# Preparing the input of two fused MLP layers in timed steps with buffers of its own, in a kernel of rotary attention and two wide layers

## The chip, the cores and the metric

One core of one Trainium2 chip. The metric is the device time of one execution in microseconds; for the kernel before it is the median of three runs. Where the text says TensorE, VectorE, ScalarE, GpSimd and SyncE, the profile's rows say PE (and PEld for its weight loads), DVE, ACT, POOL and SP.

## The reference

Attention with rotary embeddings over 4 batches, 8 heads, 576 positions and 64 dims, then two layers on the 2304 tokens of 512 dims, all in float32:

```python
q_rot, k_rot = (rotate(q), rotate(k))
scores = scale * np.matmul(q_rot, k_rot.transpose(0, 1, 3, 2))
attn = np.exp(scores - np.max(scores, axis=-1, keepdims=True))
attn = attn / (np.sum(attn, axis=-1, keepdims=True) + 1e-09)
x = (attn @ v)            # heads side by side: 2304 x 512
h = np.maximum(x @ w_in, 0.0);  x = h * h @ w_out              # layer 0, d_ff 2048
h = x @ w_in2;  x = (np.maximum(h, 0) + alpha * np.minimum(h, 0)) @ w_out2   # layer 1
```

## The kernel before

To keep float32's precision, each operand of a product is split into a high and a low part that TensorE takes at its fast rate, and a product is three matmuls: high by high, high by low, low by high. High parts are made by ACT (a copy that rounds), low parts by DVE (a subtraction).

*Attention* (`attention`) takes 16 pairs of heads, each in 9 steps of scores; a step's probabilities are transposed 4 steps later (L222, splits in L210 and L211) and the products with v (L267) follow. Unnormalised results go to `xd` in memory, the reciprocals of the sums to `rd`. From a number of steps after the last scores on (`FOLLOW`), each of its steps also lets the second part run one step further.

*The layers* (`moe`) are one list of units. A block is 384 of the 2304 tokens, so there are six; a unit is one block by one of 16 tiles of `w_in` (z = 0, L511 to L513) or `w_out` (z = 1, L529): 12 matmuls, 9 in layer 1's second half. Blocks 0 and 1 of layer 0 come first and take turns tile by tile (units 0 to 63); then each block has 32 units, blocks 2 to 5 of layer 0 (64 to 191), and all six of layer 1 (192 to 383). The loop over t issues at step t: the products of unit t, the split of g for unit t + 1 (`split_g`: gh on ACT L476, gl on DVE L477, two buffers each), the activation of unit t - 1 (`finish`: ACT relu L551, then the square on ACT L557 or POOL L559 by turns), and the jobs of the table for this t, later stages first. Steps with t < 2 run inside attention's last steps. PE, DVE, ACT and POOL keep program order from t = 2 on (`manual_schedule`; attention has it for PE alone); before that, and on SP throughout, the framework's scheduler sets the order.

*Weights* (`Weights`) arrive as float32 pairs of words that are converted in five stages at steps from a table: load two steps ahead (SP, L371), `convert` (DVE L380, L381, L382), `grow` one step later (ACT L387), `sign` two later (DVE L392, L393), `join` three later (ACT L399, L400, POOL L401). Layer 0's 32 weights come at 1.8 units each, from weight 26 on at 2 and not before unit 45, and stay in the chip's memory; layer 1's 32 are converted during blocks 2 to 5 at 2.9 units each into `wc` (two buffers), stored to memory (SP L447) and loaded back in block 5.

*The layers' input x* comes in four chunks of 128 dims a block. `prepare_x` does a chunk in one go: four loads (SP L493 xr, L495 r), add of two halves (DVE L496), product with r (POOL L497), xh (ACT L500), xl (DVE L501); for layer 1 a single load (L499) takes the place of loads, add and product. xr and r have one buffer each for blocks 0 and 1, later two for xr and one for r. Blocks 0 and 1 are prepared at t = -8 to -4; a later block's chunks at i = 4 to 7 of the z = 1 half of the block before it.

## Time and profile before

| | |
|---|---|
| median of three runs | 1254.2 us (1252.58 to 1254.74) |
| the profiled execution's own time | 1252.51 us |
| its span, first to last instruction | 1250.7 us |
| mean granted TensorE clock | 0.969 |
| busy: PE, DVE, ACT, POOL | 89%, 55%, 48%, 35% of the span |
| attention's part | to about 340 us |
| layer 0 | to about 849 us |
| layer 1 | to 1244.8 us |

A stage is read by the busy time of the engines in it and the granted clock; where TensorE is idle, the row of an instruction names in brackets how long its engine stood before it and whose end released it. An engine takes its instructions in order, so that one that waits holds all behind it.

### The profile page before, as it was taken

What the parts mean: (1) busy time and instruction counts of PE and PEld (TensorE: products, weight loads), DVE (VectorE), ACT (ScalarE), POOL (GpSimd) and SP (SyncE); (2) the same over time, 40 slices, a digit from 0 to 9 for tenths busy, and PEclk for the clock granted to TensorE, in tenths of its full rate; (3) what the DMA queues carried; (4) which work ended last, traced back from release to release, by engine and by line L of the source; (5) the groups of instructions that cost most, each with busy time, mean ns of one, the idle gap of its engine ahead of it and who ended that gap; (6) DMA issues with size and microseconds to landing.
All of it is one profiled execution on the core that took longest, in us unless ns stands there. A gap on an engine that the chain in (4) does not pass through costs nothing.

```text
span 1250.7 us, 18130 instructions
## 1 busy us (share of the span) xinstructions
PE 1118.2 (89%) x6480; PEld 1047.9 (84%) x6480; DVE 690.5 (55%) x1179; ACT 603.4 (48%) x1292; POOL 440.4 (35%) x404
## 2 busy tenths in 40 slices
PE   2899999999639878798897998999999999999998
PEld 2788988998529767798897997999898999989896
DVE  3788888888636787755756655032323232323332
ACT  2788878787516664555463553332323232322222
POOL 7965665621114442223242232103132222313040
PEclk9999999999869989999898998999999999999999
DMA  8776775654533344345655553883000101010101
GB/s 238 178 189 179 177 184 151 164 133 116 164 107 101 110 140 125 104 155 168 197 186 172 185 170 122 243 278 93 26 26 26 26 26 26 14 38 1 38 1 25
DMA packets 97497, 150.20 MB, mean 120 GB/s; under 512 B 21760, under 2 KB 66432, under 8 KB 97408
## 3 DMA queue, kind: packets, MB, share of 16 engines
q1 hardware_dynamic: 91792, 138.85, 39.1%
q10 hardware_dynamic: 5360, 10.07, 2.2%
q8 instruction: 51, 0.84, 0.3%
q14 instruction: 38, 0.31, 0.1%
q0 software_dynamic: 256, 0.13, 0.0%
HBM read 84.98 MB, written 35.73 MB: 97 GB/s over the span
## 4 chain that ended last, share of the span: by engine, by line
PE 61%; DVE 12%; POOL 8%; DMA 8%; issue 5%; ACT 5%; SPq 2%; ACTq 0%; POOLq 0%; DVEq 0%
PE py L529 24%; PE ph L511 9%; PE ph L512 9%; PE ph L513 9%; PE acc L267 3%; PE sc L201 3%; PE ps L222 2%; DVE m L381 2%; POOL xr L497 2%; DMA kraw<-in_k_dram 2%; DMA r<-r 2%; POOL w L401 2%; DMA xr<-x 2%; DVE w L382 1%; DVE ptl L211 1%
## 5 line engine op out<-in xcount | busy, mean ns | idle before, releaser
L511 PE MATMUL ph<-xh,w 128*128 128x384 f32 x768 | 260.4, 339 | 29.4 <-ACT xh L500 22.0
L512 PE MATMUL ph<-xl,w 128*128 128x384 f32 x768 | 259.5, 338 | 0.0
L513 PE MATMUL ph<-xh,w 128*128 128x384 f32 x768 | 258.7, 337 | 0.6 <-POOL w L401 0.6
L477 DVE TENSOR_TENSOR gl<-g,gh 128x384 fp32r<-128x384 f32 x192 | 109.7, 572 | 206.5 <-ACT gh L476 206.5
L555 POOL TENSOR_TENSOR g<-g,mn 128x384 f32<-128x384 f32 x96 | 100.3, 1045 | 297.1 <-DVE mn L554 297.1
L529 PE MATMUL py<-gh,w 128*128 128x384 f32 x640 | 178.6, 353 | 23.7 <-ACT gh L476 23.7
L551 ACT ACTIVATE g<-ph 128x384 f32<-128x384 f32 x192 | 93.5, 490 | 202.3 <-PE ph L513 194.7
L476 ACT ACTIVATE gh<-g 128x384 fp32r<-128x384 f32 x192 | 100.0, 521 | 184.0 <-PE py L529 151.8
L529 PE MATMUL py<-w,gh 128*128 128x512 f32 x576 | 177.4, 389 | 0.0
L511 PEld LDWEIGHTS ph<-xh,w 128*128 128x128 f32 x768 | 145.8, 190 | 33.8 <-ACT xh L500 24.0
L529 PEld LDWEIGHTS py<-gh,w 128*128 128x128 f32 x640 | 124.2, 200 | 28.3 <-ACT gh L476 28.3
L512 PEld LDWEIGHTS ph<-xl,w 128*128 128x128 f32 x768 | 145.7, 190 | 1.7 <-DVE xl L501 1.5
L513 PEld LDWEIGHTS ph<-xh,w 128*128 128x128 f32 x768 | 145.8, 190 | 0.9 <-POOL w L401 0.9
L401 POOL TENSOR_TENSOR w<-m,w 128x512 fp32r<-128x512 f32 x64 | 87.9, 1374 | 155.0 <-ACT w L399 136.0
L554 DVE TENSOR_SCALAR mn<-ph,al 128x384 f32<-128x384 f32 x96 | 59.3, 618 | 141.6 <-ACT g L551 135.9
L529 PEld LDWEIGHTS py<-w,gh 128*128 128x128 f32 x576 | 108.0, 188 | 22.2
L529 PE MATMUL py<-gl,w 128*128 128x384 f32 x320 | 115.5, 361 | 9.8 <-DVE gl L477 9.7
L205 ACT ACTIVATE p<-sc,nm 128x576 f32<-128x576 f32 x144 | 106.6, 741 | 25.7 <-DVE nm L204 18.9
L204 DVE TENSOR_REDUCE nm<-sc 128x1 f32<-128x576 f32 x144 | 105.8, 752 | 20.0 <-PE sc L201 18.6
L529 PE MATMUL py<-w,gl 128*128 128x512 f32 x288 | 112.2, 389 | 0.0
L211 DVE TENSOR_TENSOR ptl<-ps,pth 128x512 fp32r<-128x512 f32 (+1 forms) x160 | 99.7, 631 | 15.3 <-ACT pth L210 12.9
L210 ACT ACTIVATE pth<-ps 128x512 fp32r<-128x512 f32 (+1 forms) x160 | 86.9, 554 | 40.8 <-PE ps L222 40.1
(94 smaller groups left out, 1921.2 us busy)
## 6 DMA issues: line engine op xcount, KB each, us to landing
w<-in_moe_w_in_dram SPq DMA_DIRECT2D x32, 512.0 KB
w<-in_moe_w_out_dram SPq DMA_DIRECT2D x32, 512.0 KB
wk<-w SPq DMA_DIRECT2D x32, 512.0 KB
w<-wk SPq DMA_DIRECT2D x32, 512.0 KB
xr<-x SPq DMA_DIRECT2D x72, 192.0 KB
kH<-nat SPq DMA_DIRECT2D x64, 144.0 KB
qT<-nat SPq DMA_DIRECT2D x64, 144.0 KB
kL<-nat SPq DMA_DIRECT2D x64, 144.0 KB
```

The source lines that it names most:

```text
L204: V.tensor_reduce(out=nm, in_=sc[:, :, 0:SH], axis=AX.XY, op=ALU.max, negate=True)
L205: A.activation(out=Pt[n, i][:, j * S:(j + 1) * S].rearrange("p (a b) -> p a b", a=2), in_=sc[:, :, 0:SH], func=AF.Exp, bias=nm, accum_out= ...
L211: V.tensor_tensor(out=sl(lo), in0=src, in1=sl(hi).bitcast(F32), op=ALU.subtract)
L401: G.tensor_tensor(out=wc[:, 1], in0=m.bitcast(F32), in1=lo.bitcast(F32), op=ALU.mult)
L476: A.activation(out=hi, in_=g, func=AF.Copy)
L477: V.tensor_tensor(out=lo, in0=g, in1=hi.bitcast(F32), op=ALU.subtract)
L511: T.matmul(ph[:, :W], lhsT=wh[:, cs], rhs=xh, start=(c == 0), stop=False)
L512: T.matmul(ph[:, :W], lhsT=wh[:, cs], rhs=xl, start=False, stop=False)
L513: T.matmul(ph[:, :W], lhsT=wl[:, cs], rhs=xh, start=False, stop=(c == KC - 1))
L529: T.matmul(acc, lhsT=x, rhs=y, start=(s0 and k == 0), stop=(s1 and k == 2))
L551: A.activation(out=g, in_=ph, func=AF.Relu)
L555: G.tensor_tensor(out=g, in0=g, in1=mn, op=ALU.add)
```

## The change

FOLLOW is 1 instead of 5 and STEPS_AHEAD 8 instead of 7: the layers' steps begin with the second step after the last scores, at t = -9. Program order on PE, DVE, ACT and POOL begins there. `prepare_x` becomes four stages with steps of their own: `load_x`, `join_x` (the add now on POOL, but for block 0), `high_x`, `low_x`. For blocks 0 and 1 xr and r have a pool of six buffers each, which is given up at t = 2; later a pool of two each. A later block's chunks are three units apart: load at the first unit of the z = 1 half before it (block 2: four weights later) plus 3c, join two units after that, high two after the join, low one more. The raw weights have four buffers and are loaded three units ahead; the first four are converted at t = -6, -4, -2, 0 as before. `wc` has one buffer.

```diff
-FOLLOW = 5
+FOLLOW = 1
...
-STEPS_AHEAD, EARLY = 7, 2
+STEPS_AHEAD, EARLY = 8, 2
 HELD0, OUT0 = 4, 10
-EVERY0, EVERY1, EVERY2 = 1.8, 2, 2.9
+CONV0, EVERY0, EVERY1, EVERY2 = -6, 1.8, 2, 2.9
...
-        self.stages = ((-2, self.load), (0, self.convert), (1, self.grow), (2, self.sign), (3, self.join))
+        self.stages = ((-3, self.load), (0, self.convert), (1, self.grow), (2, self.sign), (3, self.join))
...
-        w64 = st.tile([P, 512, 2], U32, name="w64", bufs=3)
+        w64 = st.tile([P, 512, 2], U32, name="w64", bufs=4)
...
+        xtmp = mo.enter_context(ExitStack())
         xp = [xfirst.enter_context(tc.tile_pool(name="xp0", bufs=KC, side="right"))]
+        xp.append(xtmp.enter_context(tc.tile_pool(name="xt0", bufs=6, side="right")))
+        mo.enter_context(tc.manual_schedule(engines={ET.PE, ET.DVE, ET.Activation, ET.Pool}))
...
+        xin = {}
+
+        def load_x(layer, b, c):
+            c0 = b * W
+            xr = xp[1].tile([P, 2, W], F32, name="xr")
+            r = None
+            if layer == 0:
+                r = xp[1].tile([P, W], F32, name="r")
+                for j in range(2):
+                    nc.sync.dma_start(out=xr[64 * j:64 * j + 64],
+                                      in_=xd[j, :, c, c0:c0 + W].rearrange("(y d) c -> d y c", y=2))
+                    nc.sync.dma_start(out=r[64 * j:64 * j + 64], in_=rd[c, j:j + 1, c0:c0 + W].to_broadcast([D, W]))
+            else:
+                nc.sync.dma_start(out=xr[:, 0], in_=x2[:, c, c0:c0 + W])
+            xin[layer, b, c] = xr, r
+
+        def join_x(layer, b, c):
+            xr, r = xin[layer, b, c]
+            if layer == 0:
+                (V if b == 0 else G).tensor_tensor(out=xr[:, 0], in0=xr[:, 0], in1=xr[:, 1], op=ALU.add)
+                G.tensor_tensor(out=xr[:, 0], in0=xr[:, 0], in1=r, op=ALU.mult)
+
+        def high_x(layer, b, c):
             c0 = b * W
             if first(layer, b):
                 if b == 0:
@@ -485,21 +510,12 @@
                 xh, xl = (x[:, c0:c0 + W] for x in xsp["first"][c])
             else:
                 xh, xl = (xp[0].tile([P, W], F32R, name=nm) for nm in ("xh", "xl"))
-            xr = xp[0].tile([P, 2, W], F32, name="xr", bufs=1 if first(layer, b) else 2)
-            x = xr[:, 0]
-            if layer == 0:
-                r = xp[0].tile([P, W], F32, name="r", bufs=1)
-                for j in range(2):
-                    nc.sync.dma_start(out=xr[64 * j:64 * j + 64],
-                                      in_=xd[j, :, c, c0:c0 + W].rearrange("(y d) c -> d y c", y=2))
-                    nc.sync.dma_start(out=r[64 * j:64 * j + 64], in_=rd[c, j:j + 1, c0:c0 + W].to_broadcast([D, W]))
-                V.tensor_tensor(out=x, in0=x, in1=xr[:, 1], op=ALU.add)
-                G.tensor_tensor(out=x, in0=x, in1=r, op=ALU.mult)
-            else:
-                nc.sync.dma_start(out=x, in_=x2[:, c, c0:c0 + W])
-            A.activation(out=xh, in_=x, func=AF.Copy)
-            V.tensor_tensor(out=xl, in0=x, in1=xh.bitcast(F32), op=ALU.subtract)
+            A.activation(out=xh, in_=xin[layer, b, c][0][:, 0], func=AF.Copy)
             xsp.setdefault((layer, b), []).append((xh, xl))
+
+        def low_x(layer, b, c):
+            xh, xl = xsp[layer, b][c]
+            V.tensor_tensor(out=xl, in0=xin.pop((layer, b, c))[0][:, 0], in1=xh.bitcast(F32), op=ALU.subtract)
 
...
-        def job(at, *j):
-            for d, stage in weights.stages:
+        def job(at, stages, *j):
+            for d, stage in stages:
                 jobs.setdefault(int(at) + d, []).append((-d, stage, j))
 
+        conv = [(d, lambda *j, f=f: f(st, *j)) for d, f in weights.stages]
         for k in range(2 * FC):
-            at = -STEPS_AHEAD + 1 + EVERY0 * k if k < HELD0 else EARLY + EVERY0 * (k - HELD0)
+            at = CONV0 + EVERY0 * k if k < HELD0 else EARLY + EVERY0 * (k - HELD0)
...
-            job(at, 0, k // FC, k % FC)
-            job(at_unit[0, FIRST, 0, 0] + EVERY2 * k, 1, k // FC, k % FC)
+            job(at, conv, 0, k // FC, k % FC)
+            job(at_unit[0, FIRST, 0, 0] + EVERY2 * k, conv, 1, k // FC, k % FC)
+        for c in range(KC):
+            job(-6 + c // 2, ((-3, load_x), (0, join_x), (1, high_x), (2, low_x)), 0, 0, c)
+            job(-4 + c // 2, ((-5 if c < 2 else -3, load_x), (0, join_x), (1, high_x), (2, low_x)), 0, 1, c)
+            for layer in range(2):
+                for b in range(0 if layer else FIRST, NB):
+                    before = (layer, b - 1) if b else (layer - 1, NB - 1)
+                    job(at_unit[before + (1, 0 if before != (0, FIRST - 1) else 4)] + 3 * c + 2,
+                        ((-2, load_x), (0, join_x), (2, high_x), (3, low_x)), layer, b, c)
 
...
-        for c in range(KC):
-            prepare_x(0, 0, c)
         for t in range(-STEPS_AHEAD - 1, NU + 1):
-            if -STEPS_AHEAD <= t < -STEPS_AHEAD + KC:
-                prepare_x(0, 1, t + STEPS_AHEAD)
             if t == EARLY:
+                xtmp.close()
...
-                mo.enter_context(tc.manual_schedule(engines={ET.PE, ET.DVE, ET.Activation, ET.Pool}))
...
             if t == at_unit[0, 0, 1, 0]:
                 xfirst.close()
-                xp[0] = pool("xp1", KC, side="right")
-                late["wc"] = pool("wc", 2, side="right")
+                xp[:] = pool("xp1", KC, side="right"), pool("xt1", 2, side="right")
+                late["wc"] = pool("wc", 1, side="right")
...
             for d, stage, j in sorted(jobs.get(t, []), key=lambda x: x[0]):
-                stage(st, *j)
+                stage(*j)
...
-                nxt = (layer, b + 1) if b + 1 < NB else (layer + 1, 0)
-                if z == 1 and 4 <= i < 4 + KC and nxt[0] < 2 and not first(*nxt):
-                    prepare_x(*nxt, i - 4)
```

In the built program, POOL at the start of the layers (xr is x before its split, r the reciprocals, w a finished weight). Before, from the first product of x on:

```order
L497 TENSOR_TENSOR xr_4727<-xr_4727,r_4728 128x384
L497 TENSOR_TENSOR xr_4739<-xr_4739,r_4740 128x384
L497 TENSOR_TENSOR xr_4751<-xr_4751,r_4752 128x384
L401 TENSOR_TENSOR w_4830<-m_4795,w64_4773 128x512
L401 TENSOR_TENSOR w_4843<-m_4824,w64_4799 128x512
L497 TENSOR_TENSOR xr_4763<-xr_4763,r_4764 128x384
L401 TENSOR_TENSOR w_4882<-m_4837,w64_4828 128x512
L497 TENSOR_TENSOR xr_4775<-xr_4775,r_4776 128x384
L497 TENSOR_TENSOR xr_4785<-xr_4785,r_4786 128x384
L497 TENSOR_TENSOR xr_4801<-xr_4801,r_4802 128x384
L497 TENSOR_TENSOR xr_4812<-xr_4812,r_4813 128x384
```

Of the change, from there on (L502 the add, L503 the product, L401 the weight's join):

```order
L503 TENSOR_TENSOR xr_4647<-xr_4647,r_4648 128x384
L503 TENSOR_TENSOR xr_4653<-xr_4653,r_4654 128x384
L503 TENSOR_TENSOR xr_4678<-xr_4678,r_4679 128x384
L503 TENSOR_TENSOR xr_4684<-xr_4684,r_4685 128x384
L502 TENSOR_TENSOR xr_4659<-xr_4659 128x384
L503 TENSOR_TENSOR xr_4659<-xr_4659,r_4660 128x384
L502 TENSOR_TENSOR xr_4665<-xr_4665 128x384
L503 TENSOR_TENSOR xr_4665<-xr_4665,r_4666 128x384
L401 TENSOR_TENSOR w_4821<-m_4745,w64_4645 128x512
L502 TENSOR_TENSOR xr_4753<-xr_4753 128x384
L503 TENSOR_TENSOR xr_4753<-xr_4753,r_4754 128x384
```

The four products of block 0 now stand first, then add and product of block 1's first two chunks, and the first weight's join behind them; before, three weights' joins stood between the products.

DVE at attention's end (m is a weight's low part, w64 its raw words, ptl and pttl attention's low parts). Before, from the first weight on:

```order
L380 TENSOR_SCALAR m_4795<-w64_4773 128x512
L381 SCALAR_TENSOR_TENSOR m_4795<-w64_4773,m_4795 128x512
L211 TENSOR_TENSOR ptl_4482<-ps_4612,pth_4481 128x4x128
L211 TENSOR_TENSOR pttl_4480<-ps_4619,ptth_4479 128x384
L211 TENSOR_TENSOR ptl_4499<-ps_4627,pth_4498 128x4x128
L211 TENSOR_TENSOR ptl_4482<-ps_4634,pth_4481 128x4x64
L211 TENSOR_TENSOR pttl_4480<-ps_4643,ptth_4479 128x128
L270 COPY st0_4625<-acc_4653 128x288
L211 TENSOR_TENSOR ptl_4499<-ps_4634,pth_4498 128x4x64
L211 TENSOR_TENSOR pttl_4480<-ps_4643,ptth_4479 64x64
L496 TENSOR_TENSOR xr_4751<-xr_4751 128x384
L211 TENSOR_TENSOR pttl_4480<-ps_4643,ptth_4479 64x64
```

Of the change, from attention's last split on:

```order
L211 TENSOR_TENSOR pttl_4480<-ps_4699,ptth_4479 64x64 x2
L270 COPY st0_4625<-acc_4709 128x288
L250 TENSOR_SCALAR sums_120<-sums_120 128x9
L251 RECIPROCAL sums_120<-sums_120 128x9
L380 TENSOR_SCALAR m_4745<-w64_4645 128x512
L381 SCALAR_TENSOR_TENSOR m_4745<-w64_4645,m_4745 128x512
L382 TENSOR_SCALAR w64_4645<-w64_4645 128x512
L502 TENSOR_TENSOR xr_4647<-xr_4647 128x384
L502 TENSOR_TENSOR xr_4653<-xr_4653 128x384
L270 COPY st1_4626<-acc_4765 128x288
L502 TENSOR_TENSOR xr_4678<-xr_4678 128x384
L502 TENSOR_TENSOR xr_4684<-xr_4684 128x384
```

The first weight and all of x moved behind attention's splits; one of attention's copies (st1) now stands behind the first weight and two adds.

ACT in the second half of block 2, where x of block 3 is prepared (gh is the high part of a unit's activations). Before:

```order
L500 ACTIVATE xh_6801<-xr_6803 128x384
L476 ACTIVATE gh_6825<-g_6512 128x384
L387 ACTIVATE w64_6755<-w64_6755,pbias_62 128x512
L500 ACTIVATE xh_6832<-xr_6834 128x384
L476 ACTIVATE gh_6856<-g_6512 128x384
L500 ACTIVATE xh_6862<-xr_6864 128x384
```

Of the change:

```order
L513 ACTIVATE xh_6818<-xr_6719 128x384
L479 ACTIVATE gh_6839<-g_6519 128x384
L387 ACTIVATE w64_6751<-w64_6751,pbias_62 128x512
L479 ACTIVATE gh_6859<-g_6519 128x384
L479 ACTIVATE gh_6883<-g_6564 128x384
L399 ACTIVATE w64_6751<-w64_6751 128x512
L400 ACTIVATE w_6887<-w64_6751 128x512
L513 ACTIVATE xh_6893<-xr_6790 128x384
```

Chunks stood one or two units apart, with a weight's stages between them; now three units of gh stand between one xh and the next.

## Rows read from the trace of the kernel before

**Rows 1.** Busy time by stage: span, then engines, PE's granted clock, DMA share, GB/s.
```profile
320.00:376.90 56.90, 27.78 (x110) 22.00 (x109) 26.58 (x50) 15.91 (x32) 10.15 (x9) 0.69 0.46 134
376.90:455.00 78.10, 64.39 (x347) 61.43 (x346) 59.06 (x83) 52.09 (x99) 37.57 (x32) 0.96 0.38 113
455.00:540.50 85.50, 71.46 (x380) 66.52 (x379) 60.52 (x98) 40.30 (x74) 21.94 (x18) 0.98 0.41 125
540.50:620.90 80.40, 72.27 (x385) 69.37 (x385) 50.10 (x82) 41.01 (x78) 24.94 (x22) 0.96 0.53 168
620.90:703.00 82.10, 74.39 (x387) 71.29 (x386) 50.60 (x83) 43.20 (x82) 27.03 (x24) 0.92 0.56 182
703.00:782.40 79.40, 71.97 (x386) 68.89 (x385) 45.43 (x75) 40.33 (x77) 24.81 (x23) 0.96 0.48 160
782.40:848.90 66.50, 66.50 (x385) 66.50 (x384) 12.32 (x22) 22.99 (x46) 6.63 (x8) 1.00 0.84 261
848.90:1244.80 395.90, 395.90 (x2017) 361.65 (x2015) 125.85 (x219) 111.32 (x224) 100.33 (x96) 1.00 0.08 24
```

**Rows 2.** The chain that ended last, 340 to 378 us: start, length, what.
```profile
359.36 1.00 POOL xr L497
...
362.24 3.53 DMA xr<-x
...
366.59 1.00 POOL xr L497
...
375.31 0.69 PE ph L511
...
376.94 0.50 ACT g L551
```

**Rows 3.** Timeline of SP and DVE, attention's end: start, length, what, [idle before <-releaser].
```profile
304.55 0.63 SPq L493 DMA_DIRECT2D xr<-x  x1
...
326.65 0.43 DVE L380 TENSOR_SCALAR m<-w 128x512 uint32<-128x512 uint32 x1 [4.93 <-DMA w<-in_moe_w_in_dram]
...
332.34 0.23 DVE L211 TENSOR_TENSOR pttl<-ps,ptth 64x64 fp32r<-64x64 f32 x1
```

**Rows 4.** Timeline of DVE and ACT in the first two blocks.
```profile
418.58 0.69 DVE L392 SCALAR_TENSOR_TENSOR w<-w 128x512 uint32<-128x512 uint32 x1 [0.86 <-ACT w L387]
...
423.64 0.69 DVE L392 SCALAR_TENSOR_TENSOR w<-w 128x512 uint32<-128x512 uint32 x1 [0.87 <-ACT w L387]
...
485.06 0.66 ACT L399 ACTIVATE w<-w 128x512 f32<-128x512 f32 x1
...
502.33 0.66 ACT L399 ACTIVATE w<-w 128x512 f32<-128x512 f32 x1
```

**Rows 5.** Timeline of POOL and ACT in block 2.
```profile
591.42 0.99 POOL L497 TENSOR_TENSOR xr<-xr,r 128x384 f32<-128x384 f32 x1 [3.98 <-DMA r<-r]
...
592.44 0.52 ACT L500 ACTIVATE xh<-xr 128x384 fp32r<-128x384 f32 x1 [3.37 <-POOL xr L497]
```

**Rows 6.** Groups by line, 300 to 860 us, and two lines' durations min/median/max.
```profile
L401 POOL TENSOR_TENSOR w<-m,w 128x512 fp32r<-128x512 f32 x64 | 87.9, 1374 | 155.0 <-ACT w L399 136.0 <-issue 14.4 <-DVE gl L477 4.2
...
L381 DVE SCALAR_TENSOR_TENSOR m<-w,m 128x512 f32<-128x512 uint32 x64 | 63.1, 987 | 2.2
...
L382 DVE TENSOR_SCALAR w<-w 128x512 uint32<-128x512 uint32 x64 | 44.2, 691 | 2.1
...
L497 POOL TENSOR_TENSOR xr<-xr,r 128x384 f32<-128x384 f32 x24 | 24.0, 999 | 94.0 <-DVE xr L496 66.2 <-DMA r<-r 22.3 <-DMA r<-ri 5.6
...
L381 DVE SCALAR_TENSOR_TENSOR m<-w,m x64: 691/694/1696, 327.1 to 769.1; 128x512 f32<-128x512 uint32 x64
...
L382 DVE TENSOR_SCALAR w<-w x64: 421/428/1561, 332.6 to 769.8; 128x512 uint32<-128x512 uint32 x64
```

**Rows 7.** Timeline of SP in block 2, and the DMA's share 4.5 us later.
```profile
578.53 0.32 SPq L447 DMA_DIRECT2D wk<-w  x1
...
583.00:583.50 0.50, 0.50 (x5) 0.50 (x4) 0.50 (x2) 0.50 (x2) 0.00 (x0) 1.00 0.03 8
```

More of the change, by code (lines that the diff above doesn't have):

```diff
@@ L478, in split_g @@
             gsp[u] = hi, lo
-        def prepare_x(layer, b, c):
+        xin = {}
[18 more added lines that the diff above has]
+        def high_x(layer, b, c):
             c0 = b * W
```

## The prediction

> **What bounds the kernel now.** I read the windows by stage first, then for each stage that loses time the chain of waits or the timeline that says who is late. A block is 384 tokens, a unit is one block by one of 16 weight tiles of one matrix, 12 products in the first layer; units 0 to 63 are the first two blocks, interleaved, and each later block has 32.
>
> The measure is the sixth block of the first layer: 32 units in 66.5 us with TensorE busy throughout [rows 1], so 2.08 us a unit; the second layer, 395.9 us, is as full, and no gain is to be had in either. The losses lie between 320 and 782 us [rows 1]: the transition (27.78 us busy of 56.9, granted clock 0.69), the first two blocks (78.1 and 85.5 us, 32 units each) and blocks 2, 3 and 4 (80.4, 82.1 and 79.4 us, where 66.5 is possible).
>
> In the transition the x of the first two blocks comes one chunk after the other, since xr and r have one buffer each: POOL's product with r ends, then r and xr are loaded, then add and product. Product to product takes 366.59 - 359.36 = 7.23 us, 3.53 of it the load [rows 2]. There are eight chunks. The last releases TensorE at 375.3; unit 1's result is taken up at 376.94 [rows 2]. Attention's tail is hit too: DVE stands 4.93 us before the first weight, because its load has not landed, with attention's splits queued behind it; the last of them ends 332.34 + 0.23 [rows 3].
>
> In the first two blocks the weights are the pace: DVE joins the sign of one, converts the next, ACT grows it, and only then can DVE sign again. From sign to sign 423.64 - 418.58 = 5.06 us [rows 4], where two units take 4.16. ACT's relus and TensorE follow that loop.
>
> In blocks 2 to 4 the loss is x again. ACT makes xh as soon as its program says, but POOL's product waits 3.98 us for r; ACT waits for that (3.37 us), the gh of the next unit stands behind it, and TensorE waits for gh [rows 5].
>
> **The change, part by part.**
>
> (A) Transition. The eight chunks get buffers for six, and the table of steps puts all loads first. The raw v buffer comes free as before, so the first x load goes out at about 304.55 [rows 3]; an issue takes 0.63 us, so 16 of them end near 315, before attention does. DVE no longer meets an early xr or weight: attention's splits end about 5.6 us earlier (the wait of 4.93 and a weight step of 0.69 in front of them), near 327; a copy, the first weight's conversion and one add follow, 2.6 us as I estimate from medians of such steps, and POOL starts on x at about 329.7. From there I add POOL's queue, in the order shown: four products and four adds with four products, 12 x 1.0, and one weight join of 1.37 before unit 0 ends [rows 6]: 329.7 + 12.0 + 1.4 = 343.1; 1.4 for DVE's second pair of adds (a copy for TensorE stands between) and for the last two chunks' loads, which wait for buffers, makes 344.5. xh and xl add 1.1, and the last products of unit 1 run at the lower clock level after the pause: 347. That is 30 us before 376.94. Against it: in the old order DVE had used the wait to convert two weights more, and the weight loop sets the pace next. From my queue sum weight 3 is signed about 5 us after unit 1 instead of 1.4, so I give back 3: **27 us**. Bounds: 18, if x's loads and the weights' delay each other by one more load (3.53) and DVE's queue by one loop (5.06), to 33, if nothing is given back.
>
> (B) Block 2's x, made during the first two blocks. The joins of weights 25 and 26 stand 17.27 us apart [rows 4]; the plan has six units between them, 12.5 us. With loads ahead I take **3 us** of the 4.8 (0 to 5). The loop of 5.06 us itself is in the same order on DVE and ACT, and I give it no change; the fourth weight buffer and the load a unit earlier cost and bring nothing there, since the loop waits for engines and not for a load.
>
> (C) Blocks 2 to 4. 241.9 us now, 3 x 66.5 = 199.5 without loss: 42.4 to be had. A chunk's load now stands two units (4.16 us) before its use and a load takes 3.5; xh stands two units after add and product (2.0 us on POOL), xl one later. So no wait of that kind [rows 5] is left by order. What is added: the add goes from DVE to POOL, 12 x 1.0 us more on POOL. DVE pays when POOL works beside it: its two costliest weight steps have medians of 694 and 428 ns, but means of 987 and 691, so 0.56 us are lost beside each POOL join of 1.37 us [rows 6], 41%. Eight POOL steps of 1.0 a block then cost DVE 3.3 us; DVE is busy 50.1 us of a block [rows 1], but bunched in the half that also splits g, so I let all of it reach TensorE: 3.5 us a block stay, 10.5 in all, and **32 us** are won. By the Trainium skill's page "SBUF — State Buffer", section "SBUF: two separate sides", the port pair that DVE and POOL share is an exclusive lock: whichever is second waits for the whole instruction. That speaks against moving the add; by it 8.0 us a block would stay, and the sum would be 13.5 us worse. The 41% here are less than that, an average over steps that overlap and steps that don't. Bounds: 42 (nothing stays) to 18 (8.0 a block).
>
> (D) The second layer's converted weights go through one buffer instead of two, so ACT may write the next only when the store of the last has landed. Now nothing waits for it, so the price is bounded: the store issued at 578.53 and the load right behind it have both left the DMA engines by 583.0 [rows 7], so it lands within 4.5 us. Write 1.4 + store 4.5 is 5.9 us; the joins stand three units apart, 6.24, which hides it, and three times two units, 4.16, which is short by 1.8. Bounds 0 and 6; I take **2 us** lost, since two of the three fall where ACT works for no split of g.
>
> Sum: 27 + 3 + 32 - 2 = 60. The profiled run took 1252.51 us, 1.7 under the median of the three, 1254.2. 1254.2 - 60 = **1194 us**.
>
> **The rivals.**
>
> *The lock decides.* Each add and product blocks DVE for its full length, DVE in turn gl, and TensorE. For it: single DVE steps of up to 1561 ns against a median of 428 [rows 6]. Against: DVE has 16 us free in a block. C is then 18: 1254.2 - 46 = 1208. This is the exclusive lock of the Trainium skill's page "SBUF — State Buffer" carried to its end; the 41% above is what the trace has of it, hence the small chance.
>
> *The transition stays long.* x comes early but the weights do not: the first weight's load waits for attention's last scores, and the loop of 5.06 us starts late and paces units 0 to 31. For it: that loop ends each such unit now. Against: four weight loads stand ahead of their use. A falls to 10: 1211.
>
> *Slower.* The one weight buffer becomes the pace of blocks 2 to 5: if x's loads (3.53) stand in front of the store, write to write is 1.4 + 4.5 + 3.5 = 9.4 us against 6.03 on average (2.9 units), ACT waits with gh behind it, and 32 weights cost 32 x 3.4 = 108 us: 1254.2 - 60 + 108 = 1302. It makes the kernel slower from about 1.9 us a weight on, that is when stores take 6.5 us on average. Only 12 of the 32 have an x chunk near, and x's loads wait for buffers freed at other units, so I don't expect it.
>
> *It doesn't do what it says.* The loads could wait for older readers of the same memory, so that chunks are serial again. In the order as built, a load waits for the users of its buffer six chunks back (two, from block 2 on), so there is little for it.
>
> **How the numbers follow.** Forecast as summed 0.70; the lock 0.12; the long transition 0.08; both better than I took them (A 33, C 40) 0.04, 1181 and below; slower 0.05; no change 0.01. A measurement of this kernel tells about 0.2% (2.5 us) from no change. All but the last two are faster: 0.94, 0.01, 0.05. Range: the good ends of A and C give 33 + 5 + 40 = 78, 1176; the bad end of A with the lock gives 18 + 3 + 18 - 6 = 33, 1221, but both at once are rarer than either alone (1208, 1211). I take 1177 to 1215.
>
> **What would show it.** Right: unit 1's relu near 347, no wait of POOL's products for each other between 330 and 345; blocks 2 to 4 at 68 to 72 us, PE's clock row without the 8s and 9s there; waits of gh behind xh gone; xr and r landing before POOL reaches them; the second layer unchanged at 396 us. Wrong on (C): those blocks at 74 or more, TensorE waiting for gl from DVE, and DVE steps of 1.5 us beside POOL's adds. Wrong on (D): ACT idle before the write of wc's high half, released by a DMA. Wrong on (A): POOL idle for x loads after 331, or the weights' loop longer than 5.1 us from unit 4 on.

## The result and the profile after

| | before | after |
|---|---|---|
| median (in the same comparison) | 1253.39 us (1250.29 to 1254.74) | 1211.03 us (1205.5 to 1211.9) |
| ratio, 95% interval | | 0.9656 (0.9621 to 0.9691) |
| the profiled execution, its span | 1252.51, 1250.7 us | 1211.9, 1210.1 us |

The kernel is faster by 42 us; the forecast was 60 (1194 us, range 1177 to 1215). The profiled execution of after is the slowest of its four. The windows by stage of after, cut where the same units begin as in [rows 1] (columns as there):

```profile
320.00:363.00 43.00, 28.66 (x108) 24.10 (x107) 29.81 (x47) 16.91 (x37) 18.00 (x15) 0.57 0.55 160
363.00:437.50 74.50, 65.62 (x350) 63.31 (x348) 57.00 (x81) 49.74 (x94) 35.63 (x30) 0.95 0.36 111
437.50:522.80 85.30, 72.00 (x386) 68.93 (x386) 68.00 (x101) 43.35 (x78) 29.52 (x23) 0.96 0.47 138
522.80:596.00 73.20, 67.74 (x385) 66.28 (x384) 53.60 (x78) 41.10 (x78) 30.70 (x26) 1.00 0.56 176
596.00:669.20 73.20, 67.75 (x387) 66.48 (x386) 52.12 (x78) 41.74 (x79) 32.40 (x27) 1.00 0.62 200
669.20:741.70 72.50, 67.89 (x385) 66.28 (x384) 48.28 (x72) 41.61 (x79) 32.23 (x27) 1.00 0.54 178
741.70:808.30 66.60, 66.60 (x387) 66.60 (x386) 12.24 (x22) 22.95 (x47) 6.63 (x8) 1.00 0.82 259
808.30:1204.20 395.90, 395.88 (x2016) 361.60 (x2015) 125.83 (x219) 111.17 (x223) 100.32 (x96) 1.00 0.08 24
```

Block 5 and layer 1 stand as they stood. The transition is 14 us shorter, the first two blocks 4, blocks 2 to 4 together 23: from 80.4, 82.1 and 79.4 [rows 1] to 73.2, 73.2 and 72.5, where 66.6 is possible. POOL is busier by 5 to 7 us a block, and TensorE's clock no longer dips there (1.00 for 0.92 to 0.96). TensorE's busy time in these three blocks is 218.6 us before and 203.4 after, so some 15 of the 23 us go with the clock; the rest are waits.

**The transition.** The timeline of after at attention's end, DVE, POOL, ACT and PE (start, length, what, [idle before <-releaser]; L502 is the add of x, L503 the product, L513 xh, L518 xl, L567 the relu, L380 the first weight's first step, L387 a weight's grow):

```profile
328.02 0.23 DVE L211 TENSOR_TENSOR pttl<-ps,ptth 64x64 fp32r<-64x64 f32 x1 [0.29 <-ACT ptth L210]
...
330.67 0.43 DVE L380 TENSOR_SCALAR m<-w 128x512 uint32<-128x512 uint32 x1
...
332.20 1.02 DVE L502 TENSOR_TENSOR xr<-xr 128x384 f32<-128x384 f32 x2
336.80 0.46 DVE L270 COPY st<-acc 128x288 f32<-128x288 f32 x1 [3.58 <-PE acc L267]
337.18 1.02 DVE L502 TENSOR_TENSOR xr<-xr 128x384 f32<-128x384 f32 x2
...
332.83 2.20 POOL L503 TENSOR_TENSOR xr<-xr,r 128x384 f32<-128x384 f32 x2 [27.51 <-DVE xr L502]
337.81 2.22 POOL L503 TENSOR_TENSOR xr<-xr,r 128x384 f32<-128x384 f32 x2 [2.77 <-DVE xr L502]
...
349.27 1.25 POOL L502 TENSOR_TENSOR xr<-xr 128x384 f32<-128x384 f32 x1 [3.10 <-DMA xr<-x]
...
353.00 1.20 POOL L503 TENSOR_TENSOR xr<-xr,r 128x384 f32<-128x384 f32 x1
...
340.12 0.41 ACT L272 ACTIVATE st<-acc 128x288 f32<-128x288 f32 x1 [6.17 <-PE acc L267]
341.01 0.75 ACT L387 ACTIVATE w<-w,pbias 128x512 uint32<-128x512 uint32 x1 [0.48 <-ACT st L272]
341.67 1.75 ACT L513 ACTIVATE xh<-xr 128x384 fp32r<-128x384 f32 x4
...
361.31 0.76 ACT L387 ACTIVATE w<-w,pbias 128x512 uint32<-128x512 uint32 x1 [1.25 <-DVE w L382]
...
362.90 0.47 ACT L567 ACTIVATE g<-ph 128x384 f32<-128x384 f32 x1
...
345.06 0.69 PE L527 MATMUL ph<-xh,w 128*128 128x384 f32 x1 [4.97 <-ACT w L400]
```

The loads are early now, as forecast. But the first weight's grow and the first four xh stand on ACT behind attention's last copy, and ACT is idle 6.17 us until that can run; DVE's second pair of adds stands behind another such copy (3.58), and POOL for that (2.77). TensorE, whose products those copies wait for, runs at its lower level by then. The first two relus stand on ACT behind one more weight's grow (361.31). Unit 1's relu is at 362.90, 14.0 before the 376.94 of [rows 2].

**Blocks 2 to 4.** A unit with a chunk in block 2 of after, DVE and POOL side by side (L480 is gl, L401 the weight's join):

```profile
567.04 0.42 DVE L380 TENSOR_SCALAR m<-w 128x512 uint32<-128x512 uint32 x1
567.50 1.69 DVE L381 SCALAR_TENSOR_TENSOR m<-w,m 128x512 f32<-128x512 uint32 x1
569.22 1.12 DVE L382 TENSOR_SCALAR w<-w 128x512 uint32<-128x512 uint32 x1
570.26 1.36 DVE L480 TENSOR_TENSOR gl<-g,gh 128x384 fp32r<-128x384 f32 x1
571.54 0.55 DVE L518 TENSOR_TENSOR xl<-xr,xh 128x384 fp32r<-128x384 f32 x1
572.01 0.55 DVE L480 TENSOR_TENSOR gl<-g,gh 128x384 fp32r<-128x384 f32 x1
...
567.18 1.45 POOL L401 TENSOR_TENSOR w<-m,w 128x512 fp32r<-128x512 f32 x1 [3.87 <-ACT w L399]
568.60 1.45 POOL L502 TENSOR_TENSOR xr<-xr 128x384 f32<-128x384 f32 x1
570.13 1.07 POOL L503 TENSOR_TENSOR xr<-xr,r 128x384 f32<-128x384 f32 x1
...
571.67 0.44 PE L545 MATMUL py<-gl,w 128*128 128x384 f32 x1 [1.36 <-DVE gl L480]
```

No row waits for x any more. But the three DVE steps beside POOL take 1.69, 1.12 and 1.36, and without POOL beside them 0.69, 0.43 [rows 6] and 0.55 (the next gl here). They end as if each had begun when POOL's step ended: 567.18 + 1.45 + 0.69 = 569.32 (569.19 in the row), 568.60 + 1.45 + 0.43 = 570.48 (570.34), 570.13 + 1.07 + 0.55 = 571.75 (571.62). All 56 DVE steps of blocks 2 to 4 that take over 0.15 us more than they do alone end so, each within 0.15 us. POOL's add is stretched in turn, 1.45 here against 1.0 for such a step. gl comes late, and TensorE waits for it. Over blocks 2 to 4 that is the one large wait of TensorE (the waits view, 524.9 to 743.8: total, times, longest):

```profile
PE py L545 <- DVE gl L480: 15.5, 12, 1.4
```

Twelve chunks, twelve waits. Before, the same view (540.5 to 782.4) had the waits for gh as the large ones:

```profile
PE py L529 <- ACT gh L476: 19.2, 12, 2.9
PE py L529 <- DVE gl L477: 3.9, 12, 1.1
```

POOL's groups of the three blocks (count, busy us, mean ns, idle before):

```profile
L502 POOL TENSOR_TENSOR xr<-xr 128x384 f32<-128x384 f32 x12 | 16.5, 1377 | 0.4 <-DMA xr<-x 0.3
L503 POOL TENSOR_TENSOR xr<-xr,r 128x384 f32<-128x384 f32 x12 | 12.9, 1079 | 0.9
```

The add takes 1.38 us on average, the product 1.08, and neither waits for more than 1 us in all.

### The profile page after: what moved, and what is told of

It is laid out like the page before. It is cut to its first block, busy times and chain, and to the rows that moved or that the text cites. A ratio compares the mean times of both kernels' runs of the same rounds, so it can differ in the third digit from the quotient of the medians.

```text
span 1210.1 us, 18112 instructions
## 1 busy us (share of the span) xinstructions
PE 1105.9 (91%) x6480; PEld 1044.5 (86%) x6480; DVE 705.4 (58%) x1159; ACT 603.1 (50%) x1292; POOL 470.4 (39%) x424
## 4 chain that ended last, share of the span: by engine, by line
PE 65%; DVE 14%; issue 5%; POOL 5%; ACT 5%; DMA 4%; SPq 2%; ACTq 0%; POOLq 0%; DVEq 0%
PE py L545 24%; PE ph L528 9%; PE ph L529 9%; PE ph L527 9%; PE acc L267 5%; PE sc L201 4%; PE ps L222 3%; DVE m L381 2%; DVE gl L480 2%; DMA qraw<-in_q_dram 2%; POOL w L401 2%; DVE w L382 1%; DVE nat L144 1%; DVE ptl L211 1%; DVE nm L204 1%
## 5 line engine op out<-in xcount | busy, mean ns | idle before, releaser
L480 DVE TENSOR_TENSOR gl<-g,gh 128x384 fp32r<-128x384 f32 x192 | 121.4, 633 | 207.2 <-ACT gh L479 207.2
L567 ACT ACTIVATE g<-ph 128x384 f32<-128x384 f32 x192 | 93.4, 489 | 198.4 <-PE ph L529 190.9
L545 PE MATMUL py<-gh,w 128*128 128x384 f32 x640 | 167.0, 337 | 2.9 <-ACT gh L479 2.9
L401 POOL TENSOR_TENSOR w<-m,w 128x512 fp32r<-128x512 f32 x64 | 89.8, 1403 | 146.1 <-ACT w L399 129.2
L545 PE MATMUL py<-gl,w 128*128 128x384 f32 x320 | 109.8, 343 | 21.0 <-DVE gl L480 21.0
L545 PEld LDWEIGHTS py<-gh,w 128*128 128x128 f32 x640 | 117.0, 189 | 3.2 <-ACT gh L479 3.2
```

The source lines that it names most:

```text
L401: G.tensor_tensor(out=wc[:, 1], in0=m.bitcast(F32), in1=lo.bitcast(F32), op=ALU.mult)
L480: V.tensor_tensor(out=lo, in0=g, in1=hi.bitcast(F32), op=ALU.subtract)
L545: T.matmul(acc, lhsT=x, rhs=y, start=(s0 and k == 0), stop=(s1 and k == 2))
L567: A.activation(out=g, in_=ph, func=AF.Relu)
```

## The experiments

All are edits of the kernel after. Where a run tells about the transition it is read by the first relu (unit 0), where about blocks by the time from one block's first relu to the next one's:

| run | median us | ratio to before, 95% | relu, unit 0 | relu, unit 64 | blocks 2, 3, 4 | block 5 |
|---|---|---|---|---|---|---|
| after | 1211.03 | 0.9656 (0.9621 to 0.9691) | 361.97 | 524.85 | 73.3, 73.1, 72.6 | 66.6 |
| no_join | 1192.42 | 0.9523 (0.9478 to 0.9568) | 361.28 | 522.43 | 67.3, 68.5, 68.3 | 66.6 |
| no_add | 1198.92 | 0.9584 (0.9550 to 0.9617) | 357.63 | 518.25 | 70.1, 71.2, 70.4 | 66.6 |
| add_dve | 1199.56 | 0.9578 (0.9538 to 0.9618) | 361.41 | 523.48 | 68.5, 71.6, 71.1 | 66.6 |
| every38 | 1202.10 | 0.9603 (0.9570 to 0.9636) | 357.85 | 520.72 | 70.0, 71.0, 70.0 | 67.3 |
| free_order | 1200.66 | 0.9583 (0.9553 to 0.9614) | 346.73 | 514.42 | 73.3, 73.4, 72.4 | 66.6 |
| follow_m1 | 1209.68 | 0.9656 (0.9627 to 0.9685) | 358.84 | 521.78 | 73.4, 73.2, 72.6 | 66.6 |
| loads_two_ahead | 1211.87 | 0.9674 (0.9645 to 0.9702) | 361.25 | 524.25 | 73.3, 73.2, 72.6 | 66.6 |
| loads_two_wc2 | 1211.03 | 0.9661 (0.9617 to 0.9705) | 359.51 | 522.53 | 73.4, 73.5, 72.5 | 66.6 |
| pe_free | 1206.19 | 0.9642 (0.9621 to 0.9663) | 356.27 | 519.40 | 72.7, 73.4, 72.4 | 66.6 |
| pe_written | 1200.19 | 0.9591 (0.9571 to 0.9610) | 344.16 | 512.85 | 73.3, 73.2, 72.6 | 66.6 |
| both_parts | 1184.92 | 0.9471 (0.9450 to 0.9491) | 345.99 | 513.00 | 68.1, 68.8, 67.3 | 67.3 |
| early_joins | 1186.48 | 0.9476 (0.9451 to 0.9501) | 347.42 | 516.63 | 67.0, 68.3, 67.0 | 68.8 |

The first four edits leave the transition as it is in after, and their unit 0 still comes anywhere from 357.6 to 361.4: the transition of one and the same order varies by some 4 us between executions. Smaller differences there mean nothing. Each run has its ratio from its own comparison, in which before took 1251.5 to 1253.5 us; by the ratios most gains over after come out 1 to 3 us smaller than by the medians.

**The rest in blocks 2 to 4: no_join, no_add, add_dve, every38.** My theory after the result was that DVE and POOL stretch each other; the rivals were the weights' loop with its one `wc`, and late transfers.

```diff
# no_join: both steps for blocks 0 and 1 alone
-            if layer == 0:
+            if layer == 0 and b < FIRST:
```

> Left out: add and product of x in blocks 2 to 5 of layer 0 (blocks 0 and 1 keep them); the loads stay. Sharing theory: blocks 2 to 4 take 73.2, 73.2 and 72.5 us instead of the 66.6 of block 5 because POOL's add (1.33) and product (1.10) and DVE's work beside them stretch each other, so without them a block takes 66.6 to 67.5 us, L381 falls back from 1.0 to about 0.8 mean, and the time is 1190 to 1195 us. Rival, weights' loop (one wc buffer, store before the next join): nothing of that is touched, blocks stay at 72 to 73, 1208 to 1212 us. Rival, x transfers late: loads are the same, blocks stay at 72 to 73.

```diff
# no_add
+                if b < FIRST:
-                (V if b == 0 else G).tensor_tensor(out=xr[:, 0], in0=xr[:, 0], in1=xr[:, 1], op=ALU.add)
+                    (V if b == 0 else G).tensor_tensor(out=xr[:, 0], in0=xr[:, 0], in1=xr[:, 1], op=ALU.add)
```

> Left out: only the add of x in blocks 2 to 5 of layer 0. Sharing theory: the loss follows POOL's busy time, so 1.10 of 2.43 us is left of it: 6.6 x 0.45 = 3.0 us over 66.6, blocks at 69 to 70.5, time about 1200 (1197 to 1204). If the stretch comes only where three POOL operations stand in a row, less: blocks at 67 to 68, 1193 to 1196. Rivals (weights' loop, x transfers): blocks at 72 to 73, 1208 to 1212.

```diff
# add_dve
-                (V if b == 0 else G).tensor_tensor(out=xr[:, 0], in0=xr[:, 0], in1=xr[:, 1], op=ALU.add)
+                (V if b != 1 else G).tensor_tensor(out=xr[:, 0], in0=xr[:, 0], in1=xr[:, 1], op=ALU.add)
```

> The add of blocks 2 to 5 is DVE's, as it was before the change, all else as after. Sharing theory: 0.55 us on DVE stands for 1.33 on POOL, (0.55 + 1.10) / 2.43 of the loss stays: 66.6 + 4.5 = about 71 a block, time 1203 to 1207. If DVE is a bound by itself (its own queue, not the sharing): blocks longer than 73.2, time 1212 to 1216. Rivals: no change, 1208 to 1212.

```diff
# every38
-CONV0, EVERY0, EVERY1, EVERY2 = -6, 1.8, 2, 2.9
+CONV0, EVERY0, EVERY1, EVERY2 = -6, 1.8, 2, 3.8
```

> The second layer's weights are converted every 3.8 units instead of 2.9, so they reach into block 5 and 3.2 instead of 4.1 of them fall beside the 12 units with x chunks. Sharing theory: one conversion costs about 2.7 us of DVE and 1.0 of POOL when alone, so one fewer saves 3 to 3.6 us a block: blocks 2 to 4 at 69.5 to 70.5, block 5 at 66.6 to 68, time 1200 to 1204. Rival, x's own chain (transfers, the two xr buffers): no change, 1208 to 1212. Rival, weights' loop with one wc buffer: a gain too, down to 66.6 a block, about 1192, since the loop would not come to wait at this pace.

Windows of block 3 (from first relu to first relu) of after:

```profile
598.15:671.27 73.12, 67.67 (x386) 66.40 (x385) 51.53 (x77) 41.90 (x79) 32.68 (x27) 1.00 0.61 199
```

of no_join:

```profile
589.75:658.24 68.49, 67.43 (x386) 66.36 (x385) 48.95 (x79) 42.39 (x79) 22.22 (x19) 1.00 0.64 208
```

of no_add:

```profile
588.31:659.56 71.25, 67.95 (x386) 66.35 (x385) 50.77 (x79) 41.97 (x80) 27.96 (x23) 1.00 0.63 210
```

and of add_dve:

```profile
591.94:663.56 71.62, 69.41 (x386) 67.99 (x385) 53.75 (x84) 42.36 (x80) 28.26 (x23) 0.98 0.66 216
```

Without add and product the three blocks take 68.0 us on average for 73.0; TensorE's waits for gl over them fall from 15.5 to 2.1 us. The same loads are moved, so late transfers are out, and the weights' loop is as it was. Without the add alone it is 70.6. So some 10 us of POOL's time a block cost TensorE 5.0, and 4.5 of them (the add) cost 2.4: about half, each time. DVE's busy time tells the same: over the three blocks it is 152.6 us in after and 138.5 in no_join, 14.1 less, where the blocks are 14.9 shorter. The add put back on DVE, where it had been, costs no more than leaving it out (70.4): DVE does it in 0.55 us and no POOL step stands against it. The blocks are close to where the theory put them (71), but blocks 3 and 4 of this trace have a clock of 0.98 and TensorE is busy 2.9 us more over the three than in no_add; without that I estimate 69.5, so the add on DVE costs less than the theory has it. The profiled execution (1202.76 us) is the slowest of its four, and the median is under the forecast (1203 to 1207). In every38 the blocks come to 70.3, as expected by the sharing (though a weight's join takes 1.3 us on POOL when alone, not the 1.0 counted there); a `wc` that decided would have given 66.6. Its interval and that of after overlap, and the blocks of its trace carry this point. The 1.4 us a block that no_join leaves over 66.6 I put down to the weights' joins, which it keeps (L381 still takes up to 1.70 us beside them); no run leaves these out, so that is argued and not shown.

**The transition: free_order, follow_m1.** The theory is that the written order on DVE and ACT costs the time. One rival is that the clock and the first weight's path set it whatever the order; the other side is that the written order is the gain.

```diff
# free_order
-        mo.enter_context(tc.manual_schedule(engines={ET.PE, ET.DVE, ET.Activation, ET.Pool}))
...
             if t == EARLY:
...
+                mo.enter_context(tc.manual_schedule(engines={ET.PE, ET.DVE, ET.Activation, ET.Pool}))
```

> As after, but from the last scores to unit 2 the framework's scheduler orders the engines again, as before the change; the x stages and buffers, the loads three units ahead and the early start stay. Order theory: the transition fell short because ACT's first grow and xh stand behind attention's last copy (340.12) and DVE's second pair of adds behind the other (336.80); set free, relus 0 and 1 come at 350 to 358 instead of 361.97 and 362.90, blocks 2 to 4 stay at 73, time 1200 to 1208. Clock and transfer rival: PE's lower clock from 326.6 on and the first weight's path set it whatever the order, relus within 2 us of 362, 1208 to 1213. Other side: the written order is where the 14 us came from, the scheduler spreads the x work over attention's tail and attention ends later; relu 1 at 368 to 377, time 1216 to 1226.

```diff
# follow_m1
-FOLLOW = 1
+FOLLOW = -1
```

> The layers' first steps come two of attention's steps earlier in program order (FOLLOW -1 for 1), nothing else. Order theory: the first weight's DVE part, the first adds and the first xh then stand ahead of attention's last copies (333.54 to 340.12) and not behind them; relu 0 moves from 361.97 to 355 to 358, all else by the same, time 1204 to 1207. Clock and transfer rival: relus stay at 361 to 363, 1208 to 1213. Other side: DVE and ACT are what attention's last pieces wait for, so attention's last copy comes at 344 instead of 340 and relu 0 at 364 to 367, 1214 to 1217.

The free order is worth 10.4 us by the medians, 9 by the ratios, and unit 0 comes 15.2 earlier. ACT's timeline in it (lines from 500 on are one lower than in after, so L512 is xh, L566 the relu):

```profile
321.83 0.54 ACT L512 ACTIVATE xh<-xr 128x384 fp32r<-128x384 f32 x1
...
327.45 0.52 ACT L512 ACTIVATE xh<-xr 128x384 fp32r<-128x384 f32 x1
...
330.88 0.77 ACT L387 ACTIVATE w<-w,pbias 128x512 uint32<-128x512 uint32 x1 [0.60 <-DVE xr L501]
...
338.36 0.41 ACT L272 ACTIVATE st<-acc 128x288 f32<-128x288 f32 x1 [2.64 <-PE acc L267]
...
347.69 0.47 ACT L566 ACTIVATE g<-ph 128x384 f32<-128x384 f32 x1
```

Six of the eight xh (313.42 to 334.64) and the first grow stand ahead of the last copy, in after none, and POOL's first product of x starts at 312.37 instead of 332.83. Unit 1's relu is at 347.69. Its first x load goes out at 306.76, in after at 305.35 (SP's timelines), so the loads are not what differs. Two steps earlier in the written order (follow_m1) change the median by 1.4 us and unit 0 by 3.1, less than the transition varies, and not the 4 to 7 us that the order theory asked for. Yet the first grow, and four xh behind it, do stand ahead of ACT's last copy there:

```profile
333.14 0.77 ACT L387 ACTIVATE w<-w,pbias 128x512 uint32<-128x512 uint32 x1 [0.48 <-DMA w<-in_moe_w_in_dram]
...
343.05 0.41 ACT L272 ACTIVATE st<-acc 128x288 f32<-128x288 f32 x1 [7.50 <-PE acc L267]
```

The copy itself comes 2.9 us later than in after, near the 344 of the other side. That speaks against the order theory in this form: the place of these steps behind the copy is not by itself what the written order costs.

**Which engines' order: pe_free, pe_written.** The free order also mixes attention's last products with its transposes on TensorE, so the engines were set free apart.

```diff
# pe_free (pe_written: {ET.PE} in this place); at t == EARLY all four, as in free_order
-        mo.enter_context(tc.manual_schedule(engines={ET.PE, ET.DVE, ET.Activation, ET.Pool}))
+        mo.enter_context(tc.manual_schedule(engines={ET.DVE, ET.Activation, ET.Pool}))
```

> As after, but from the last scores to unit 2 the scheduler orders TensorE alone; DVE, ACT and POOL keep the written order. If TensorE's own order cost the 10 us that the free order gave (attention's last value products all behind its last transposes, so that TensorE waits and falls to the lower clock at 320 to 330): relu 0 at 346 to 350, time 1200 to 1204. If the order of DVE and ACT cost them (adds, grow and xh behind attention's last copies): relu 0 at 360 to 363, time 1208 to 1213. Half each: between.

> The opposite: in the same stretch TensorE alone keeps the written order, and DVE, ACT and POOL are the scheduler's. If TensorE's order is the cause: relu 0 at 358 to 363, time 1206 to 1212. If the order of DVE and ACT is: relu 0 at 346 to 350, time 1200 to 1204.

The windows at attention's end of after:

```profile
320.00:330.00 10.00, 6.76 (x40) 5.71 (x38) 5.38 (x12) 4.86 (x13) 0.00 (x0) 0.78 0.95 249
330.00:340.00 10.00, 8.22 (x31) 7.29 (x31) 4.39 (x11) 0.68 (x2) 4.40 (x5) 0.50 0.64 209
340.00:350.00 10.00, 4.43 (x12) 3.33 (x12) 8.07 (x11) 5.63 (x11) 6.74 (x7) 0.50 0.39 112
```

and of pe_written:

```profile
320.00:330.00 10.00, 6.51 (x45) 5.11 (x44) 8.49 (x20) 6.58 (x16) 1.99 (x2) 1.00 0.90 268
330.00:340.00 10.00, 7.42 (x47) 6.90 (x46) 8.05 (x13) 5.50 (x12) 5.94 (x5) 1.00 0.80 222
340.00:350.00 10.00, 6.85 (x22) 6.23 (x21) 4.41 (x9) 4.21 (x9) 3.27 (x4) 0.66 0.51 170
```

With TensorE's order as written and the others free, the whole gain is there (1200.19, unit 0 at 344.16). With TensorE alone free it is 1206.19, and its interval overlaps that of after; what TensorE's order is worth stays open. So the order on DVE, ACT and POOL cost the 8 to 11 us (by ratio and by median). Between 330 and 340 ACT works 5.50 us instead of 0.68, and TensorE runs at its full level (1.00) instead of 0.50. But the order alone doesn't set these two. In no_add every engine's order is that of after up to 400 us, and its window is:

```profile
330.00:340.00 10.00, 3.65 (x24) 2.95 (x22) 6.01 (x10) 4.45 (x9) 8.24 (x8) 0.91 0.70 228
```

Its unit 0 is at 357.63, 4.3 before that of after and 13.5 behind that of pe_written. So some 4 us of unit 0 go with the clock that an execution got in this stretch, and the larger part stays with the order. Which steps in it matter was not taken apart.

**The small parts: loads_two_ahead, loads_two_wc2.**

```diff
# loads_two_ahead; loads_two_wc2 has the last line as well
-        self.stages = ((-3, self.load), (0, self.convert), (1, self.grow), (2, self.sign), (3, self.join))
+        self.stages = ((-2, self.load), (0, self.convert), (1, self.grow), (2, self.sign), (3, self.join))
-        w64 = st.tile([P, 512, 2], U32, name="w64", bufs=4)
+        w64 = st.tile([P, 512, 2], U32, name="w64", bufs=3)
-                late["wc"] = pool("wc", 1, side="right")
+                late["wc"] = pool("wc", 2, side="right")
```

> The doubles are loaded two units ahead into three buffers, as before the change; all else as after. As forecast for this part (no gain by itself): blocks 2 to 4 at 73, first two blocks 163, time 1208 to 1213. Rival, it is what shortened the weights' loop (weights 25 to 26 now 11.7 us apart, 17.27 before): first two blocks 165 to 168, time 1213 to 1217.

> As the run with loads two units ahead, and the space goes into a second buffer for the second layer's converted weights (wc), as before the change. Sharing theory: 0 to 1 us (ACT waited for wk's store 1.7 us in three times, POOL 6.3 in three, none of them on PE's path): blocks 2 to 4 at 72 to 73, within 2 us of its sibling. Rival, the one buffer holds the weights' loop up and so the blocks: 67 to 70 a block, 9 to 18 us less than its sibling.

Neither moves anything: 0.9674 and 0.9661 beside 0.9656, all inside each other's intervals.

**A faster kernel: both_parts, early_joins.** both_parts is free_order, add_dve and every38 together.

> The free order of the transition, the add of blocks 2 to 5 on DVE and the second layer's weights every 3.8 units. Sharing theory: beside 12 units with chunks (25.0 us of TensorE) stand 4 x (0.55 + 0.55 + 1.10) of x, 12 x 0.56 of gl and 3.2 x 3.6 of conversions, 27.0 us, so a block takes 66.6 + 2 = 68.6 (68 to 69.5) and block 5 67.3; with the free order's 514 at unit 64 the time is 1186 to 1191. If the two edits of the blocks save the same time twice (floor at 70): 1192 to 1195.

```diff
# early_joins, on top
-                        ((-2, load_x), (0, join_x), (2, high_x), (3, low_x)), layer, b, c)
+                        ((-2, load_x), (0, join_x), (2, high_x), (3, low_x)) if c > 1 else
+                        ((-9 - c, load_x), (-6, join_x), (2, high_x), (3, low_x)), layer, b, c)
```

> As both_parts, and the first two chunks of a block are loaded and joined before the output units of the block ahead begin (steps 3 of units before, where DVE has no gl), the last two as before. Sharing theory: 2 x 1.65 us leave the stretch, 23.7 us stand beside 25.0, a block takes 66.6 to 67.6, time 3 to 6 us under its sibling, 1181 to 1186. Rival, POOL's squares and the relus behind them pay for it in the hidden units: within 1.5 us of its sibling.

both_parts takes 1184.92 us, 26 less than after (23 by the ratios) and just under its forecast, with blocks at 68.1, 68.8 and 67.3: the two edits add up, and it beats both kernels. early_joins gets its blocks down by 1.9 us in all, not by 3 to 6, and block 5 is 1.5 longer: no gain, near the number of its rival (1.6 us from its sibling), and why block 5 pays was not looked into.

## Why the prediction was right, and where not

The sign, the places and the order of size were right, and 1211 is inside the range, 4 us from its slow end. (At the other end the bound of 33 for A is a slip: with nothing given back it is 30, which moves that end from 1176 to 1179.) Between the profiled executions 40.6 us came of the 60 (1252.51 - 1211.9): 14.0, 3.7 and 23.0 by the parts below.

**(A) Transition, 27 forecast, 14 measured: mis-sized by the order.** At unit 1 the forecast was 30, with 3 given back later. Unit 1 was to be taken up at 347 and was at 362.90, 15.9 late. POOL began on x at 332.83 instead of 329.7 (3.1). From there x took until 353.00 + 1.20 = 354.2, 21.4 us instead of 14.8 (6.6): 2.77 for the adds behind DVE's copy, where I had allowed 1.4 for this and the loads together, 3.10 for a load that waited for its buffer, and 2.0 by which POOL's steps took longer than I had them. The remaining 8.7 instead of 2.5 (6.2) are xl beside POOL, units 0 and 1 at the lower clock level, and a grow in front of the relus. The step that failed was the sum over POOL's queue alone: the waits of DVE and ACT for attention's last copies (3.58 and 6.17) and their place in the chain were in it only as 1.4 for DVE's adds and the last loads and 1.1 for xh and xl, and ACT's grow in no term. Some 4 us of the 15.9 go with the clock of the profiled execution, as no_add has unit 1 at 358.55 in the same order. One of my signs against A came: POOL idle for x loads after 331 (3.10). The free order puts unit 1 at 347.69, so the separate buffers can give what I forecast for them; the new program order takes it away. There, too, the weights' pace gives something back, as I had allowed (3): units 0 to 64 take 167.7 us instead of 162.9.

**(B) Block 2's x, 3 forecast, 3.7 measured** (17.76 at unit 64, 14.04 of it from the transition). ACT's timeline of after has the joins of weights 25 and 26 at 468.94 and 480.65, 11.7 us apart; 17.27 before [rows 4]:

```profile
468.94 0.67 ACT L399 ACTIVATE w<-w 128x512 f32<-128x512 f32 x1 [0.68 <-DVE w L393]
...
480.65 0.66 ACT L399 ACTIVATE w<-w 128x512 f32<-128x512 f32 x1
```

The gap closed by 5.6, more than the 4.8 I had counted, and 3.7 is what the first two blocks gained in all, so that 3 and 3.7 agree so well is partly luck. The load a unit earlier brings nothing, as said.

**(C) Blocks 2 to 4, 32 forecast, 23 measured: mis-sized.** What was to go went: no wait for r, none of gh behind xh [rows 5]. What was to stay was 3.5 us a block and is 6.4. Two things are in it. x's add and product on POOL cost 5.0 a block (no_join): they last 1.38 and 1.08 us on average, not 1.0, as DVE stretches them too, and about half of that time reaches TensorE, not the 41% I took from means over all stages. The other 1.4 I did not have at all; the weights' joins on POOL, which stretch DVE also without x, are my reading of it. By the Trainium skill's page "SBUF — State Buffer", section "SBUF: two separate sides", the port pair that DVE and POOL share is an exclusive lock. The single rows above agree with it, within 0.15 us. The 8.0 a block of the rival did not come of it: x's part is 5.0, nearer to my 3.5. Nearly all of POOL's x time (28.7 of 29.5 us over the three blocks) has a DVE row beside it, but it lengthens DVE's work by 14.1 only: in the unit shown, add and product take 2.52 us and cost DVE's two steps 0.69 and 0.81. Two of my three signs against C came, TensorE's waits for gl and the long DVE steps; the third did not, as the blocks at 73 lie between my 72 and 74. And the 23 that were won came by less waiting and by a clock without dips, which I had not told apart. The add was the avoidable part: on POOL it costs 2.4 to 2.6 us a block, some 7.5 in all, that DVE would not have cost.

**(D) One wc, 2 lost forecast, nothing measured** (loads_two_wc2). The waits I had named are there (for the store of wk ACT stands 1.7 us and POOL 6.3, three times each), but the second buffer given back changes no block by more than 0.3 us beside loads_two_ahead. The slower rival, built on it, falls with it.

The two milder rivals' numbers, the lock's 1208 and the long transition's 1211, lie next to the result, but each had taken the other term as forecast, so that is luck. The lock's mechanism is in the rows, at about half its price. The long transition came (A at 14, the rival had 10), but not by the rival's mechanism: DVE has the first weight at 330.67, with no wait for its load, and in pe_written, where the same loads meet another order on the engines, the first grow is at 327.09 instead of 341.01. That both terms fell short I had called rarer than either alone.

## What to carry to other kernels

Before work is moved from VectorE to GpSimd, look at what VectorE does at that very moment: where the instructions of the two stand side by side, count GpSimd's time as VectorE's for a bound, and add both up against the stage (here about half of it was lost). A written order across two parts of a program is only as good as its joint: go through every in-order engine there, and ask of each first instruction of the new part which last instruction of the old part stands ahead of it and what that waits for.

## What the runs showed of the hardware

Where DVE's steps stood beside POOL's in blocks 2 to 4, the two took turns whole instruction by whole instruction (56 of 56 stretched steps, within 0.15 us): a bitwise step with a single input went from 0.43 to 1.12 us, a subtraction from 0.55 to 1.36, and POOL's add from 1.0 to 1.45.

TensorE's clock in one stretch was not the same from execution to execution of one order: from 330 to 340 us it was granted 0.50, its lower level of 1.2 GHz, for all of it in after and 0.91 in no_add, whose order is the same on every engine up to there. With the other engines ordered freely and TensorE's order unchanged it was 1.00 (pe_written). In after it had begun to fall in the stretch before (0.78, with 6.76 us busy); in pe_written it was full there (1.00, with 6.51 us busy). And the same transition came out up to 4 us apart in runs whose program was the same up to there, the two with the higher clock from 330 to 340 (no_add, 0.91, and every38, 0.84) being the early ones.
